# Router logits of a fused attention and mixture-of-experts kernel: from split weights on the full array to fp32 on four column tiles

## The chip, the cores and the metric

The kernel runs on one core of one Trainium2 chip. The metric is the device time of one execution in microseconds (us). Before the change it is 520.21 us, the median of three runs (519.32 to 525.32).

## The reference

An attention with pooled keys and values makes x, a two-level router picks one of 16 experts for each row of x, and that expert's two matrices are applied. Everything is fp32.

```python
k_p = k.reshape(B, H, Sp, 8, D).mean(axis=3)      # B=8, H=8, S=576, D=64, Sp=72
v_p = v.reshape(B, H, Sp, 8, D).mean(axis=3)
attn = softmax(q @ k_p.T / sqrt(D));  x = (attn @ v_p) as [B*S, 512]
g_logits = x @ w_group                            # 4 groups, argmax g, softmax weight g_w
e_logits = x @ w_expert[g]                        # 4 experts in the group, argmax e, weight e_w
out[row] = g_w * e_w * (relu(x @ w1[g, e]) @ w2[g, e])   # w1 512x1024, w2 1024x512
```

## The kernel before, in words

The work goes by batch (8 of 576 rows). For each batch, `Att` makes x transposed, in two halves of the rows (256 and 320 columns in batches 0 to 2, 288 and 288 later), and `Moe` runs one expert over the whole batch: the one that most rows chose, or for batches 0 and 1 a guess. Rows that chose another expert are placed by `Left` at the end, in blocks of 32; the first block is written out within the last batch, a loop at the end (L935) runs for the others, and the profiled execution takes no turn of it.

Every large matrix product is made in a one-pass fp32 form (fp32r) from a rounded high part and a low part that holds the rest: high by high, high by low, low by high. `cast` (L552, ScalarE) makes the high part of a weight chunk and `lo` (L557, GpSimd or VectorE) the low one. `av` (L383) makes x of a half in four PSUM banks, from which ScalarE writes the high part xt[:, 0] and `avd` (L401, VectorE) the low part xt[:, 1]. `up` (L567) is x by w1 with 12 matmuls a piece, ScalarE's relu and `upd` (L582, VectorE), which writes the low part of the hidden layer; `down` (L594) is the product by w2 in pieces of 8 matmuls of 512 columns. `up` and `down` share three PSUM buffers ("mm", pool ps_m).

The router: `rt` (L405) makes 20 logits from the weights wrs, which hold 20 high and 20 low columns, by eight fp32r matmuls a half that add up in PSUM; ScalarE copies 40 rows to lt; `route_g` (L432) transposes lt by five TensorE instructions, and two VectorE reductions add the two kinds of columns. `route_e` makes the choice oh, on GpSimd where its argument is "p", and `count` (L456) adds it up on TensorE.

What sets the order: each engine runs its instructions in the order of the plans START, FIRST, SECOND, STEADY and LAST (L36 to L77), lists of pieces. `m.` is the expert work of the batch, `n.` and `a.` the attention of the next and the first batch, `x.` the one after, `w.` the next expert's weights, `l.` the leftover rows; FIRST runs batch 0 with the attention of batch 1, SECOND batch 1, STEADY batches 2 to 6, LAST batch 7. All engines follow the plan (MANUAL, L78), but ScalarE's order in LAST is left to a scheduler. An instruction that waits holds all behind it on its engine. In FIRST GpSimd folds the values of batch 1 (`n.vr`, `n.vm`: lines 274 to 292), which `guess_x` (L480, TensorE) reads to guess batch 1's expert.

Of the kernel before, what the change touches and what calls it, by code (L numbers as in the profile page):

```python
# [69 lines left out]
m.load:2:3 m.lo:1:2:v l.step l.step m.load:2:2 m.up:0:0 p.tail m.up:0:1 m.upd:0:1 m.upd:0:0 l.step l.step l.step m.up:1:0 m.up:1:1 m.upd:1:0  # L70
l.step l.step l.step l.step l.xtiles m.upd:1:1 m.up:2:0 l.step l.step l.step l.step m.upd:2:0 l.step l.step m.up:2:1 m.upd:2:1 l.step
m.up:3:0 m.up:3:1 m.up:5:0 m.upd:3:0 l.step m.lo:1:3 m.upd:3:1 m.up:4:0 l.step l.which m.upd:4:0 m.split:2:2:v m.upd:5:0 m.split:2:1:v
m.up:6:0 m.upd:6:0 m.up:5:1 m.up:4:1 m.up:6:1 m.split:2:0 l.fetch_x l.tiles m.upd:5:1 m.upd:4:1 m.upd:6:1 l.slots m.down:0 m.down:1 l.fetch_a:1
# [891 lines left out]
```

## Time and profile before

| what | us |
|---|---|
| median of three runs | 520.21 |
| the profiled execution, its own time | 520.39 |
| its span, first to last instruction | 518.7 |
| TensorE matmul busy in the span | 502.9 (97%) |
| VectorE, ScalarE, GpSimd busy | 329.5, 206.3, 255.5 |
| granted TensorE clock, mean over the span | 0.996 |

PE is TensorE, DVE VectorE, ACT ScalarE, POOL GpSimd, SP the queue that issues most DMAs. A matmul's duration runs into the next one's, so a piece of PE work is measured here from its first start to the start of the next piece. An fp32 matmul that is not a transpose stands in the trace as two instructions.

### The profile page before, as it was taken

The numbers are of one execution on the slowest core, as the hardware profiler recorded it, in microseconds if no ns is written. First come the engines' busy times: TensorE is split into PE (matmuls) and PEld (weight loads), VectorE is DVE, ScalarE is ACT, GpSimd is POOL, SyncE is SP. The second block draws the span as 40 slices with busy tenths as digits, with TensorE's granted clock in tenths as the row PEclk, the third lists the DMA queues.
The fourth block names the chain that finished last, engine by engine and source line by source line (L and its number), as shares of the span: only waits on it lengthen the run. The fifth ranks groups of instructions, "written<-read, shape, count | busy, mean of one in ns | idle before, by whom it ended". The sixth has DMA issues, their size and how long they took to land.

```text
span 518.7 us, 14903 instructions
## 1 busy us (share of the span) xinstructions
PE 502.9 (97%) x6061; PEld 444.4 (86%) x6061; DVE 329.5 (64%) x928; ACT 206.3 (40%) x384; POOL 255.5 (49%) x235
## 2 busy tenths in 40 slices
PE   8799999999999999999999999999999999999995
PEld 7698877998789988898889988898889988889874
DVE  6887878798385765486664766385664763278602
ACT  2454342544226441545244542455334551344211
POOL 2394766565518632785049541685148760322400
PEclk9999999999999999999999999999999999999998
DMA  8699298585337942778164941997356101834741
GB/s 282 185 265 196 55 261 230 106 211 127 63 122 238 257 79 86 240 232 139 38 201 159 263 74 46 346 324 133 57 163 195 56 3 38 274 105 178 239 153 37
DMA packets 118126, 83.74 MB, mean 161 GB/s; under 512 B 71034, under 2 KB 93818, under 8 KB 117800
## 3 DMA queue, kind: packets, MB, share of 16 engines
q1 hardware_dynamic: 113424, 75.70, 54.3%
q10 hardware_dynamic: 4600, 7.02, 3.9%
q8 instruction: 49, 0.80, 0.7%
q14 instruction: 21, 0.17, 0.1%
q0 software_dynamic: 32, 0.04, 0.0%
HBM read 77.31 MB, written 28.53 MB: 204 GB/s over the span
## 4 chain that ended last, share of the span: by engine, by line
PE 81%; DVE 7%; DMA 4%; ACT 2%; POOL 2%; issue 1%; SPq 1%; DVEq 0%; ACTq 0%; POOLq 0%
PE mm L578 32%; PE mm L605 29%; PE mm L622 5%; PE sc L394 4%; PE sc L334 4%; PE tp L412 3%; DMA sw<-in_moe_w_dram 3%; DMA vv<-in_v_dram 1%; POOL w L561 1%; ACT w L555 1%; POOL p L373 1%; DVE pT L380 1%; DVE mx L346 1%; DVE p L355 1%; PE tp L436 1%
## 5 line engine op out<-in xcount | busy, mean ns | idle before, releaser
L605 PE MATMUL mm<-w,ht 128*128 128x512 f32 x768 | 177.4, 383 | 0.0
L561 POOL TENSOR_TENSOR w<-sw,w 128x1024 fp32r<-128x1024 f32 (+2 forms) x87 | 149.1, 1732 | 44.0 <-ACT w L555 39.7
L605 PEld LDWEIGHTS mm<-w,ht 128*128 128x128 f32 x768 | 141.4, 189 | 21.8 <-issue 1.6
L578 PE MATMUL mm<-xb,w 128*128 128x288 f32 (+1 forms) x768 | 109.5, 294 | 1.6 <-issue 0.8
L578 PEld LDWEIGHTS mm<-xb,w 128*128 128x128 f32 x768 | 100.6, 189 | 5.2 <-ACT w L555 2.2
L578 PE MATMUL mm<-xa,w 128*128 128x288 f32 (+1 forms) x768 | 100.8, 283 | 1.7 <-ACT xa L399 0.8
L578 PEld LDWEIGHTS mm<-xa,w 128*128 128x128 f32 x768 | 95.5, 190 | 4.8 <-issue 1.7
L580 ACT ACTIVATE ht<-mm 128x288 fp32r<-128x288 f32 (+2 forms) x128 | 51.8, 410 | 88.2 <-PE mm L578 86.7
L555 ACT CAST w<-sw 128x1024 fp32r<-128x1024 f32 x64 | 66.6, 1041 | 29.6 <-DMA sw<-in_moe_w_dram 27.3
L373 POOL TENSOR_TENSOR p<-p,su 128x864 f32<-128x864 f32 (+2 forms) x30 | 40.3, 1344 | 69.8 <-DVE su L368 54.0
L591 DVE SCALAR_TENSOR_TENSOR ht<-mm,ht 128x64 fp32r<-128x64 f32 (+4 forms) x192 | 37.9, 252 | 29.9 <-ACT ht L580 29.8
L616 ACT ACTIVATE y<-mm,gm 128x512 f32<-128x512 f32 x31 | 21.2, 685 | 70.8 <-PE mm L605 70.8
L513 POOL TENSOR_TENSOR mp<-oh,moh 128x80 f32<-128x80 f32 x8 | 2.8, 355 | 84.9 <-DVE moh L478 81.5
L360 ACT ACTIVATE p<-p 128x864 f32<-128x864 f32 (+2 forms) x30 | 23.4, 781 | 36.2 <-DVE p L355 31.0
L380 DVE STREAM_TRANSPOSE pT<-p 128x960 f32<-128x960 f32 (+2 forms) x30 | 29.2, 975 | 8.6 <-POOL p L373 7.9
L586 DVE SCALAR_TENSOR_TENSOR ht<-mm,ht 128x288 fp32r<-128x288 f32 (+1 forms) x64 | 27.0, 423 | 10.8 <-ACT ht L580 10.8
L366 DVE TENSOR_REDUCE s<-p 128x12 f32<-128x864 f32 (+2 forms) x30 | 25.8, 861 | 7.0 <-ACT p L360 7.0
L334 PEld LDWEIGHTS sc<-kT,qT 64*32 64x32 f32 x2176 | 23.6, 105 | 7.0 <-issue 4.0
L334 PE MATMUL sc<-kT,qT 64*32 64x72 f32 x2176 | 28.5, 229 | 1.1 <-DVE qT L320 1.1
L622 PE MATMUL mm<-w,ht 128*128 128x512 f32 x128 | 29.4, 381 | 0.0
L394 PE MATMUL sc<-pT,v 32*64 32x288 f32 (+2 forms) x384 | 26.9, 409 | 1.2 <-DVE pT L380 1.2
L346 DVE TENSOR_REDUCE mx<-sc 128x12 f32<-128x864 f32 (+2 forms) x28 | 24.3, 868 | 5.6 <-PE sc L334 5.6
(212 smaller groups left out, 523.0 us busy)
## 6 DMA issues: line engine op xcount, KB each, us to landing
sw<-in_moe_w_dram SPq DMA_DIRECT2D x72, 512.0 KB
vv<-in_v_dram SPq DMA_DIRECT2D x27, 320.0 KB
q<-in_q_dram SPq DMA_DIRECT2D x112, 72.0 KB
kv<-in_k_dram SPq DMA_DIRECT2D x14, 512.0 KB
out_dram<-y ACTq DMA_DIRECT2D x23, 256.0 KB
xscr<-xa SPq DMA_DIRECT2D x5, 1152.0 KB
xscr<-xb SPq DMA_DIRECT2D x5, 1152.0 KB
pT<-xscr SPq DMA_DIRECT2D x4, 1152.0 KB
```

What stands on the lines that cost most here:

```text
L334: nc.tensor.matmul(ps[x][32 * g:32 * g + 32, SP * t:SP * t + SP], lhsT=s.qT[c][64 * x:64 * x + 64, g, 32 * t:32 * t + 32], rhs=s.kT[64 * x ...
L346: red(out=m[:, x, 0:w], in_=ps[:, :, 0:SP * w].rearrange("p x (t s) -> p x t s", s=SP), axis=AX.X, op=ALU.max)
L373: (nc.vector if eng == "v" else nc.gpsimd).tensor_tensor(out=p, in0=p, in1=bc(s.su[c][:, 0:w], SP), op=ALU.mult)
L380: nc.vector.transpose(out=s.pT[:, :, o:o + n].rearrange("p j (t i) -> p t j i", i=32), in_=probs[:, z:z + n // 32].rearrange("p t (j i) -> ...
L394: nc.tensor.matmul(banks[a][64 * x:64 * x + 64, 0:n], lhsT=s.v6[32 * a:32 * a + 32, 5 if x and i == 0 else j, :], rhs=s.pT[32 * a:32 * a + ...
L555: nc.scalar.copy(out=s.w[m, j][0], in_=raw)
L561: (nc.vector if eng == "v" else nc.gpsimd).tensor_tensor(out=wl[:, i:i + n], in0=s.raw[m, j][:, i:i + n], in1=wh[:, i:i + n].bitcast(F32), ...
L578: nc.tensor.matmul(ps[:, 0:n], lhsT=l[:, kc, fs], rhs=apart(s.a.xt[hf][:, r, kc]), start=(kc == 0 and i == 0), stop=(kc == 3 and i == 2))
L580: nc.scalar.activation(out=halves(ht[:, sl]), in_=joined(ps[:, 0:n]), func=AF.Relu)
L591: stt(out=ht[:, at:at + hi - lo], in0=ps[:, a, lo:hi], scalar=0.0, in1=ht[:, t + lo:t + hi].bitcast(F32), op0=ALU.max, op1=ALU.subtract)
L605: nc.tensor.matmul(ps, lhsT=s.ht[f][:, 640 * l + o:640 * l + o + 128], rhs=apart(s.w[2, f // 2][r][:, f % 2, :]), start=(i == 0), stop=(i ...
L622: nc.tensor.matmul(ps, lhsT=s.ht[f][:, 512:640], rhs=apart(s.w[2, f // 2][r][:, f % 2, :]), start=(i == 0), stop=(i == 15))
```

## The change

The router's weights stay fp32 and padded to 32 columns a tile (wr, 128x4x32). `rt` makes, for each of the four 128-row chunks of x, one fp32 matmul on its own 32 columns of the array, without adding up: four matmuls a half in place of eight. They read xr, a new fp32 copy of x. `route_g` transposes lt as five full 128x128 blocks into two PSUM tiles and VectorE adds the four chunks.

In batches 1 to 7 `avd` writes x to xr straight from PSUM, and a new piece `xlo` on GpSimd makes the low part as xr minus the high part. In batch 0 `avd` makes the low part as before, and `xlo` on GpSimd makes xr as high plus low. The piece that split the router's weights goes, the pool of pT has one buffer instead of two, and two small memsets are new on GpSimd.

ScalarE's order in LAST is written out: each `split` becomes a `cast` and a `lo`. `p.tail`, the last rows of the batch before, comes after the first two pieces of `up`. The last chunk of the last batch (`ending`) is made as two halves of 256 columns, one after the other, each scaled by ScalarE and stored. The final loop stands in an If.

```diff
-t.warm:10 t.turn_wr a.kr:0 a.kr:1 t.split_wr a.kt ...
+t.warm:10 t.turn_wr a.kr:0 a.kr:1 a.kt ...
 ...
-m.up:5:0 a.pt:4 n.vr:0 m.upd:5:0 ... m.up:7:0 a.av:1 n.vr:1 n.vm a.rt:0 m.upd:7:0 a.avd:1 n.kr:0
-m.up:0:1:1 m.upd:0:1 n.kr:1 a.rt:1 n.guess_x ...
+m.up:5:0 a.pt:4 n.vr:0 a.xlo:0 m.upd:5:0 ... m.up:7:0 a.av:1 n.vr:1 n.vm a.rt:0 m.upd:7:0 a.avd:1 a.xlo:1 n.kr:0
+m.up:0:1:1 m.upd:0:1 n.kr:1 n.guess_x m.cast:2:0 m.up:1:1 a.rt:1 n.guess_e ...
 ...
-MANUAL = [{ET.PE, ET.SP, ET.DVE, ET.Activation, ET.Pool}, {ET.PE, ET.SP, ET.DVE, ET.Pool}]
+MANUAL = {ET.PE, ET.SP, ET.DVE, ET.Activation, ET.Pool}
 ...
-    wr = keep.tile([128, 4, 20], F32, name="wr")
-    wrs = keep.tile([128, 4, 40], F32R, name="wrs")
+    wr = keep.tile([128, 4, 32], F32, name="wr")
+    nc.gpsimd.memset(wr, 0.0)
+    lt = keep.tile([128, 640], F32, name="lt")
+    nc.gpsimd.memset(lt[:, S:640], 0.0)
 ...
-    pp = ctx.enter_context(tc.tile_pool(name="pp", bufs=2))
+    pp = ctx.enter_context(tc.tile_pool(name="pp", bufs=1))
 ...
         def avd(s, h):
+            o, n = s.half[h]
             for ps, g in s.ta[h]:
-                stt(out=s.xt[h][:, 1, g], in0=ps, scalar=0.125, in1=s.xt[h][:, 0, g].bitcast(F32), op0=ALU.mult, op1=ALU.subtract)
+                if s.b == 0:
+                    stt(out=s.xt[h][:, 1, g], in0=ps, scalar=0.125, in1=s.xt[h][:, 0, g].bitcast(F32), op0=ALU.mult, op1=ALU.subtract)
+                else:
+                    ts(out=s.rawt()[:, g, o:o + n], in0=ps, scalar1=0.125, scalar2=None, op0=ALU.mult)
+
+        def xlo(s, h, eng="p"):
+            o, n = s.half[h]
+            x, hi = s.xt[h], s.xt[h][:, 0].bitcast(F32)
+            e = nc.vector if eng == "v" else nc.gpsimd
+            if s.b == 0:
+                e.tensor_tensor(out=s.rawt()[:, :, o:o + n], in0=hi, in1=x[:, 1].bitcast(F32), op=ALU.add)
+            else:
+                e.tensor_tensor(out=x[:, 1], in0=s.rawt()[:, :, o:o + n], in1=hi, op=ALU.subtract)
 
         def rt(s, h):
 ...
-            for i in range(8):
-                nc.tensor.matmul(ps[0:40, 0:n], lhsT=wrs[:, i // 2, :], rhs=apart(s.xt[h][:, i % 2, i // 2]), start=(i == 0), stop=(i == 7))
-            nc.scalar.copy(out=halves(s.lt[0:40, sl]), in_=joined(ps[0:40, 0:n]))
+            for a in range(4):
+                nc.tensor.matmul(ps[32 * a:32 * a + 32, 0:n], lhsT=wr[:, a, :], rhs=s.xr[:, a, o:o + n], start=True, stop=True)
+            nc.scalar.copy(out=lt[:, o:o + n], in_=ps[:, 0:n])
 ...
-            for c, (o, n) in enumerate(CH):
-                nc.tensor.transpose(out=lp[0:n, 40 * c:40 * c + 40], in_=s.lt[0:40, o:o + n], identity=ident[0:40, 0:40])
+            lp = [ps_t.tile([128, 512], F32, name="tp") for i in range(2)]
+            for c in range(NC):
+                nc.tensor.transpose(out=lp[c // 4][:, 128 * (c % 4):128 * (c % 4) + 128], in_=lt[:, 128 * c:128 * c + 128], identity=ident)
 ...
+            if s.b == B - 1 and c == 3:
+                return s.ending(o, t)
 ...
-                if s.b == B - 1 and c == 3:
-                    ts(out=y[:, 256:512], in0=joined(ps)[:, 1], scalar1=s.a.gm[:, c:c + 1], scalar2=None, op0=ALU.mult)
-                    nc.scalar.activation(out=y[:, 0:256], in_=joined(ps)[:, 0], func=AF.Copy, scale=s.a.gm[:, c:c + 1])
 ...
+            for i in range(16 * t, 16 * t + 16):
+                a, (f, l, r) = i // 24, ops[i % 24]
+                nc.tensor.matmul(s.pe[a][:, 0:256], lhsT=s.ht[f][:, 640 * l + o:640 * l + o + 128], rhs=apart(s.w[2, f // 2][r][:, f % 2, 256 * a:256 * a + 256]),
+                                 start=(i % 24 == 0), stop=(i % 24 == 23))
+                if i % 24 == 23:
+                    part = s.ye[:, 256 * a:256 * a + 256]
+                    nc.scalar.activation(out=halves(part), in_=joined(s.pe[a][:, 0:256]), func=AF.Copy, scale=s.a.gm[:, 3:4])
+                    (nc.sync if a else nc.scalar).dma_start(out=out[S * s.b + o:S * s.b + o + 128, 256 * a:256 * a + 256], in_=part)
 ...
-    with tc.For_i(0, nit, 1):
-        left.block()
+    with tc.If(nit > 0):
+        with tc.For_i(0, nit, 1):
+            left.block()
```

On TensorE in FIRST, from the second `av` of batch 0 (L394, L395 in the new file) to the transposes of its logits; L412 is `rt` before and L428 after, L484 and L499 `guess_x`. Before:

```order
L394 MATMUL tp<-pT,v_341 64x320 x4
L412 MATMUL tp<-xa,wrs 40x256 x8
L578 MATMUL mm<-xb,w 128x320 x12
L412 MATMUL tp<-xb,wrs 40x320 x8
L484 MATMUL tp<-heads,v_741 64x4 x10
L578 MATMUL mm<-xb,w 128x320 x12
L492 MATMUL tp<-wr,gx 128x20 x4
```

and with the change:

```order
L395 MATMUL tp<-pT,v_341 64x320 x4
L428 MATMUL tp<-xr,wr 32x256 x4
L593 MATMUL mm<-xb,w 128x320 x12
L499 MATMUL tp<-heads,v_741 64x4 x10
L593 MATMUL mm<-xb,w 128x320 x12
L428 MATMUL tp<-xr,wr 32x320 x4
L507 MATMUL tp<-wr,gx 128x20 x4
```

The second `rt` moved behind the guess and one piece of `up`; the first one stayed, and now reads xr.

On GpSimd at the same place (L275 to L293 in the new file are the folds of batch 1's values, L420 is `xlo` of batch 0), with the change:

```order
L275 TENSOR_TENSOR vv<-vv 128x2x256
L276 TENSOR_TENSOR vv<-vv 128x2x128
L288 TENSOR_TENSOR v_741<-vv 128x128
L420 TENSOR_TENSOR xr<-xa 128x4x256
L275 TENSOR_TENSOR vv<-vv 128x3x256
L276 TENSOR_TENSOR vv<-vv 128x3x128
L288 TENSOR_TENSOR v_741<-vv 128x192
L293 TENSOR_TENSOR v_741<-v_741,share 128x64 x2
L420 TENSOR_TENSOR xr<-xb 128x4x320
L469 TENSOR_TENSOR oh<-o_930,o_964 128x80
```

Without the two rows of L420 the row order is that of before: the first stands ahead of the second fold, the second behind it.

On VectorE at the start of LAST (L640 and L666 are the tail's addition, the next four lines `upd` of the first two pieces). Before:

```order
L698 COPY kv<-tp 128x320 x2
L640 TENSOR_TENSOR y<-mm,y 64x512
L591 SCALAR_TENSOR_TENSOR ht<-mm,ht 128x144
L591 SCALAR_TENSOR_TENSOR ht<-mm,ht 128x80
L591 SCALAR_TENSOR_TENSOR ht<-mm,ht 128x64
L586 SCALAR_TENSOR_TENSOR ht<-mm,ht 128x288
```

and with the change:

```order
L724 COPY kv<-tp 128x320 x2
L606 SCALAR_TENSOR_TENSOR ht<-mm,ht 128x144
L606 SCALAR_TENSOR_TENSOR ht<-mm,ht 128x80
L606 SCALAR_TENSOR_TENSOR ht<-mm,ht 128x64
L601 SCALAR_TENSOR_TENSOR ht<-mm,ht 128x288
L666 TENSOR_TENSOR y<-mm,y 64x512
```

The tail's addition, which empties a PSUM buffer, went behind the three and one instructions that empty the two of `up`.

## Rows read from the trace of the kernel before

**Rows 1.** The page: busy time of each engine, share of the span, instructions.
```profile
PE 502.9 (97%) x6061; PEld 444.4 (86%) x6061; DVE 329.5 (64%) x928; ACT 206.3 (40%) x384; POOL 255.5 (49%) x235
```
**Rows 2.** Windows over one steady batch: busy by engine, clock, DMA share, GB/s.
```profile
243.90:277.60 33.70, 33.70 (x310) 28.94 (x311) 18.64 (x56) 11.69 (x22) 12.45 (x10) 1.00 0.45 127
277.60:302.50 24.90, 24.90 (x410) 23.56 (x408) 17.96 (x41) 13.32 (x23) 18.12 (x13) 1.00 0.80 202
```
**Rows 3.** Timeline of PE, the router's matmuls in a steady batch: start, duration, instruction.
```profile
248.58 1.17 PE L412 MATMUL tp<-xa,wrs 128*40 128x288 f32 x8
249.59 1.89 PE L605 MATMUL mm<-w,ht 128*128 128x512 f32 x8
251.32 1.14 PE L412 MATMUL tp<-xb,wrs 128*40 128x288 f32 x8
252.30 3.62 PE L605 MATMUL mm<-w,ht 128*128 128x512 f32 x16
```
**Rows 4.** Timeline of PE in LAST: fp32 matmuls on four column tiles.
```profile
497.53 1.93 PE L844 MATMUL tp<-sw,q 128*32 128x256 f32 x32
499.40 0.92 PE L605 MATMUL mm<-w,ht 128*128 128x512 f32 x3
```
**Rows 5.** Timeline of PE: the logits' transposes, and five full ones of the keys.
```profile
255.85 0.47 PE L436 MATMUL tp<-ident,lt 40*128 40x40 f32 x5
256.25 0.48 PE L605 MATMUL mm<-w,ht 128*128 128x512 f32 x1
...
263.49 0.60 PE L297 MATMUL tp<-ident,kb 128*128 128x128 f32 x4
...
263.95 0.46 PE L605 MATMUL mm<-w,ht 128*128 128x512 f32 x1
```
**Rows 6.** Timeline of POOL in FIRST.
```profile
40.68 1.82 POOL L274 TENSOR_TENSOR vv<-vv 128x768 f32<-128x768 f32 x1
...
44.77 0.81 POOL L292 TENSOR_TENSOR v<-v,share 128x64 f32<-128x64 f32 x2
54.45 0.33 POOL L454 TENSOR_TENSOR oh<-o,o 128x80 f32<-128x80 f32 x1 [8.87 <-DVE o L425]
```
**Rows 7.** Groups of POOL's instructions over the span: shape, count, busy us, mean ns.
```profile
L561 POOL TENSOR_TENSOR w<-sw,w 128x1024 fp32r<-128x1024 f32 x43 | 102.8, 2397 | 34.9 <-ACT w L555 34.9
```
**Rows 8.** Timeline of PE in FIRST, the same stretch.
```profile
41.18 1.07 PE L412 MATMUL tp<-xa,wrs 128*40 128x256 f32 x8
...
44.03 1.25 PE L412 MATMUL tp<-xb,wrs 128*40 128x320 f32 x8
45.21 0.95 PE L484 MATMUL tp<-heads,v 128*64 128x4 f32 x20
```
**Rows 9.** Timeline of PE: the second `av` of batch 1 and the wait before it.
```profile
86.19 0.50 PE L394 MATMUL sc<-pT,v 32*64 32x320 f32 x4 [1.15 <-DVE pT L380]
```
**Rows 10.** Timeline of POOL, the end of FIRST.
```profile
90.49 1.68 POOL L275 TENSOR_TENSOR vv<-vv 128x384 f32<-128x384 f32 x1
...
96.81 0.33 POOL L454 TENSOR_TENSOR oh<-o,o 128x80 f32<-128x80 f32 x1 [2.84 <-DVE o L425]
```
**Rows 11.** Timeline of PE at the start of SECOND.
```profile
96.69 2.84 PE L578 MATMUL mm<-xa,w 128*128 128x256 f32 x24
99.37 0.35 PE L459 MATMUL tp<-oh,ones 128*128 128x80 f32 x2
```
**Rows 12.** Timeline of PE, ACT and DVE at the start of LAST.
```profile
456.42 1.71 PE L578 MATMUL mm<-xa,w 128*128 128x288 f32 x12
456.53 0.41 ACT L580 ACTIVATE ht<-mm 128x288 fp32r<-128x288 f32 x1
...
456.97 0.59 DVE L591 SCALAR_TENSOR_TENSOR ht<-mm,ht 128x144 fp32r<-128x144 f32 x3 [0.70 <-ACT ht L580]
```
**Rows 13.** Timeline of all engines, the end.
```profile
512.37 0.48 DVE L611 TENSOR_SCALAR y<-mm,gm 128x256 f32<-128x256 f32 x1 [1.26 <-PE mm L605]
...
512.88 0.47 ACT L612 ACTIVATE y<-mm,gm 128x256 f32<-128x256 f32 x1 [3.65 <-DVE y L611]
```

More of the change, by code (lines that the diff above doesn't have):

```diff
@@ L62 @@
 m.up:4:0 m.upd:4:0 n.ex:2 m.up:4:1 m.upd:4:1 n.su_:2 n.nm:2:p x.load_qb:0 x.load_qb:1 m.up:5:0 m.upd:5:0 m.cast:2:2 m.lo:2:2 m.up:5:1 m.upd:5:1 n.pt:2
-x.load_qb:2 x.load_qb:3 m.up:6:0 m.upd:6:0 m.up:7:0 m.cast:2:3 m.lo:2:3 m.upd:7:0 n.av:0 n.avd:0 m.up:6:1 m.upd:6:1
-m.up:7:1 m.upd:7:1 n.av:1 n.rt:0 n.avd:1
+x.load_qb:2 x.load_qb:3 m.up:6:0 m.upd:6:0 m.up:7:0 m.cast:2:3 m.lo:2:3 m.upd:7:0 n.av:0 n.avd:0 n.xlo:0 m.up:6:1 m.upd:6:1
+m.up:7:1 m.upd:7:1 n.av:1 n.rt:0 n.avd:1 n.xlo:1
 m.down:0 n.rt:1 x.kr:0 m.down:1 x.kr:1 m.down:2 n.route m.down:3 m.down:4 m.down:5 n.main_expert w.load:1:0 w.load:1:1 w.load:1:2 w.load:1:3
@@ L69 @@
 LAST = """
[L70 to L73, printed above, removed]
+m.load:2:3 m.lo:1:2:v l.step l.step m.load:2:2 m.up:0:0 m.up:0:1 m.upd:0:1 m.upd:0:0 p.tail l.step l.step l.step m.up:1:0 m.up:1:1 m.upd:1:0
+l.step l.step l.step l.step l.xtiles m.upd:1:1 m.up:2:0 m.cast:2:1 l.step l.step l.step l.step m.upd:2:0 l.step l.step m.up:2:1 m.upd:2:1 l.step
+m.up:3:0 m.up:3:1 m.up:5:0 m.upd:3:0 l.step m.lo:1:3 m.cast:2:2 m.upd:3:1 m.up:4:0 l.step l.which m.upd:4:0 m.lo:2:2:v m.upd:5:0 m.lo:2:1:v
+m.up:6:0 m.cast:2:0 m.upd:6:0 m.up:5:1 m.up:4:1 m.up:6:1 m.lo:2:0 m.cast:2:3 l.fetch_x l.tiles m.upd:5:1 m.upd:4:1 m.upd:6:1 l.slots m.down:0 m.down:1 l.fetch_a:1
 m.up:7:0 l.fetch_b:1 m.upd:7:0 l.whole:4 l.whole:0 m.up:7:1 l.rows l.next_ l.whole:3 m.upd:7:1 l.turn:3 l.turn:4 m.down:12
-l.whole:1 l.turn:1 l.turn:0 l.whole:2 m.split:2:3:p m.down:2 m.down:3 l.turn:2 m.down:4 l.gather m.down:5 l.back m.down:6 l.up m.down:7 l.hback
+l.whole:1 l.turn:1 l.turn:0 l.whole:2 m.lo:2:3:p m.down:2 m.down:3 l.turn:2 m.down:4 l.gather m.down:5 l.back m.down:6 l.up m.down:7 l.hback
 m.down:8 l.down l.fetch_x l.fetch_a l.fetch_b m.down:13 m.down:9 m.down:10 l.slots m.down:11
 """
-MANUAL = [{ET.PE, ET.SP, ET.DVE, ET.Activation, ET.Pool}, {ET.PE, ET.SP, ET.DVE, ET.Pool}]
+MANUAL = {ET.PE, ET.SP, ET.DVE, ET.Activation, ET.Pool}
 @with_exitstack
@@ L633, in down, with ending @@
                 s.store(c, "a")
+        def ending(s, o, t):
+            ops = [(f, l, r) for f in range(8) for l, r in ((0, 0), (0, 1), (1, 0))]
+            if t == 0:
+                s.pe = [ps_m.tile([128, 512], F32, name="mm") for i in range(2)]
+                s.ye = sm.tile([128, DM], F32, name="y")
+            for i in range(16 * t, 16 * t + 16):
[6 more added lines that the diff above has]
+                    (nc.sync if a else nc.scalar).dma_start(out=out[S * s.b + o:S * s.b + o + 128, 256 * a:256 * a + 256], in_=part)
         def tail(s):
@@ L784, in xtiles @@
         def xtiles(s):
-            s.xh = [pp.tile([128, 5, S], F32, name="pT")[:, 0:NG] for i in range(2)]
+            s.xh = [pp.tile([128, 5, S], F32, name="pT")[:, 0:NG], xp.tile([128, NG, S], F32, name="xr")]
             for t in s.xh:
@@ L924, in run @@
                 getattr(who[who_], fn)(*[int(z) if z.isdigit() else z for z in args])
-    with tc.manual_schedule(engines=MANUAL[0]):
+    with tc.manual_schedule(engines=MANUAL):
         run(START, 0)
```

40 lines of the change are left out of this document (16 added, 24 removed).

## The prediction

> **What bounds the kernel now.** First the page's busy shares: TensorE is busy 502.9 of 518.7 us, no other engine over 64% [rows 1]. Busy matmul time alone proves little, so the second view is the windows over one steady batch: in both stretches TensorE is busy for the whole window at full granted clock, while VectorE has 36.6 of 58.6 us and GpSimd 30.6 [rows 2]. Third, the timeline of starts: eight `down` matmuls take 1.73 us from first start to the next piece, 0.216 each, and pieces follow without a gap [rows 3]. So TensorE's own work sets the time, and a change counts by what it takes off TensorE and by the waits it puts in front of TensorE. For the waits I read GpSimd's timeline in FIRST, where it is the engine that others wait for.
>
> The profiled execution took 520.39 us and the median is 520.21, so the two may be used alike; the sum is made from 520.39.
>
> **Part 1, the logits' matmuls.** A half's eight matmuls take 1.01 us (248.58 to 249.59) and 0.98 us (251.32 to 252.30), 0.1225 each [rows 3]. The trace has the new form elsewhere: 128x32 fp32 matmuls with 256 columns in the leftover block, 16 of them (32 records) in 1.87 us from first start to the next piece [rows 4], so four, one per column tile, take 0.47 us, and at 288 columns 0.53. That they run side by side is in that number: one fp32 matmul of 256 columns alone cannot be 0.117 us if a one-pass one of 288 takes 0.1225. The lower bound is four of the old matmuls, 0.49 us. The upper bound takes the price of a change of tile shape on top: 16 `down` matmuls ahead of the 40-row transposes take 3.55 us (252.30 to 255.85), where 16 at 0.216 are 3.46 [rows 3, 5], so 0.09 more, 0.62 us a half. But the eight `down` ahead of the old logits, whose tile is narrow too, paid nothing (1.73 us for eight, 249.59 to 251.32) [rows 3]. I take 0.55. Saved: 0.995 less 0.55, times 16 halves, **7.1 us** (bounds 6.0 and 8.1). All of it is on the path, since TensorE has no gaps there.
>
> On this the Trainium skill, "TensorEngine Tiling (Array Packing)", Key Properties, says that a change of the tiling mode, not only of the tile, drains the engine. By that rule every half would pay, 0.62 us, and the saving would be 6.0 us. The trace agrees for one of the two narrow shapes and disagrees for the other.
>
> **Part 2, the transposes.** Five of 40 rows take 0.40 us and pay the 0.09 of their shape; five full ones take 0.46 us (263.49 to 263.95) [rows 5]. Per batch 0.03 less, 0.2 us in all. VectorE's two reductions read twice the elements, some tenths of a us a batch, with 22 us idle in a steady batch [rows 2]; counted at nothing. `avd` loses its wait for ScalarE; its durations stay about the same; nothing.
>
> **Part 3, `xlo` on GpSimd.** 1024 elements a partition take 2.40 us there, 2.34 ns each [rows 7]. A pair is 2.7 us twice in the steady batches, 5.4 on 30.6 us in 58.6 [rows 2]: hidden, as the next batch's `up` reads the low part a whole `down` later. If that cover went, it would show as `up` waiting for GpSimd.
>
> In FIRST it isn't hidden. GpSimd is on a row without idle until 44.77 + 0.81 = 45.58 us and only then idle for 8.87 us [rows 6].
> - The first `rt` stands at 41.18 us [rows 8] and reads xr, which `xlo` starts at 40.7, behind the first fold [rows 6], and ends at 43.1: TensorE waits 1.9 us, and all of `up` behind it.
> - The rest of the folds ends 2.4 us later, at 48.0. `guess_x` stood at 45.21 [rows 8], behind an `rt` of 1.18 us that is now behind it. TensorE would come to it at 45.21 + 1.9 - 1.2 - 0.4 = 45.5 and stick in its middle until 48.0: 2.1 us.
> - The second `rt` waits for the `xlo` of 1280 elements, 3.0 us from 48.0, so until 51.0. TensorE is there after the end of the guess (0.6) and one piece of `up` (1.75), at 50.4: 0.6 us.
>
> Together **+4.6 us**. These waits are new, on the path, and a good half of the saving. They are least if GpSimd is faster next to an idle VectorE, and bounds are half of that and one and a half times, 2.3 and 6.9.
>
> At the end of FIRST both `xlo` of batch 1, 5.4 us, stand ahead of the last fold and of oh, which `count` waits for. GpSimd idled 2.84 us before oh at 96.81 [rows 10], and `count` at 99.37 came 2.2 us after oh was done [rows 10, 11]. 5.4 - 2.84 - 2.2: **+0.4 us** (0 to 2.5).
>
> The second `av` of batch 1 waited 1.15 us for its probabilities [rows 9]. It now comes one `down` piece and more later, 1.73 us [rows 3], so this wait goes: **-1.2 us** (0 to -1.2).
>
> **Part 4, LAST.** The first two pieces of `up` and the tail hold the three PSUM buffers. Before, the tail's addition freed one and the third piece began at 456.42 [rows 12]. Now the buffer freed first is that of the second piece, and its relu stands on ScalarE behind a weight cast, at 456.53; VectorE then needs until 456.97 + 0.59 = 457.56 [rows 12]. **+1.2 us** for TensorE (0 if ScalarE comes to it earlier).
>
> **Part 5, the end.** 48 matmuls of 256 columns in place of 24 of 512: 24 of 256 columns took 2.68 us (96.69 to 99.37) [rows 11], so 5.36 against 24 x 0.216 = 5.19: +0.2. Behind the last matmul VectorE's half ran first and ScalarE's after it, 0.48 and 0.47 us [rows 13]; now one eviction of that size is left, -0.5. The store is as long as it was. The branch around the loop takes the place of the loop's own test; nothing. The early split of the weights, two small instructions beside DMA waits, and the two memsets: nothing. One pT buffer: its next writer comes after the last reader in every plan; nothing.
>
> **Sum:** 520.4 - 7.1 - 0.2 + 4.6 + 0.4 - 1.2 + 1.2 + 0.2 - 0.5 = **517.8 us**.
>
> **Rivals.**
> *The new waits don't bind.* If xr of batch 0 is ready in time, or TensorE's later pieces make up for it, parts 3 and 4 lose 4.6 + 0.4 + 1.2: 511.6 us. For it: VectorE's and ScalarE's waits in FIRST give back some of any delay. Against: GpSimd's rows leave no hole before 45.58 us [rows 6].
>
> *GpSimd slows down beside VectorE.* 384 elements took 1.68 us while VectorE folded keys, 4.4 ns each, almost twice the usual [rows 10, 7]. If every `xlo` in FIRST ran so, they would last 4.5 and 5.6 us: the guess 2.1 us later, the second `rt` another 2.6, `count` up to 2.5: 517.8 + 7.2 = 525.0 us. For it: this row, at the very place. Against: it is the slowest of its kind, and the folds in FIRST's middle ran at 2.4 ns (1.82 us for 768) [rows 6]. The Trainium skill, "GPSIMD Engine Reference", Specifications, says that GpSimd shares its SBUF interfaces with VectorE and contends with VectorE instructions that have two SBUF inputs; the slow row, beside the fold of two SBUF inputs, agrees.
>
> *The four column tiles run one after the other.* Slower: each matmul of a half would take the 0.53 us of the group, 2.1 us a half, 1.1 more than now, and the sum 517.8 + 16 x (2.1 - 0.55) = 542.6 us. It decides from 0.995 us a half on. Against: rows 4 are this very form, with the tiles in the same rotation. For it only that here each tile has one matmul, not four in succession, in a group.
>
> **How the numbers follow.** Forecast 0.64, no new waits 0.16, slow GpSimd 0.16, tiles in series 0.04. The forecast's own bounds: best 517.8 - 1.0 - 2.3 - 0.4 - 1.2 = 512.9; worst 517.8 + 1.1 + 2.3 + 2.1 + 1.2 = 524.5; not all ends at once, so some 514 to 522. To leave out no more than 2 in 10 the range is 513.0 to 522.5, which takes in the near part of both middle rivals. Two per cent is about what a measurement of this kernel can tell from no change: below 509.8 faster, 0.05 (the first rival with the best price of part 1); above 530.6 slower, 0.05; within, 0.90.
>
> **What would show it.** In the new profile: L428 pieces of about 0.55 us from start to the next piece, 0.5 us off each of two a batch, and a steady batch (58.6 us before) at 57.7; waits of TensorE's L428 and L499 for POOL L420 and L293 in FIRST, near 2 us each; no wait of the second L395 of batch 1; a wait for VectorE at the third piece of `up` in LAST; one ScalarE eviction after the last matmul. Wrong would be the forecast if L428 takes over 0.7 us, if steady batches wait for L422, or if FIRST ends as early as before.

## The result, and the profile after

The changed kernel takes **526.73 us** (median of 5 runs, 525.91 to 530.25) against 520.01 for the kernel before in the same session (5 runs): the ratio is 1.0134, 95% interval 1.0104 to 1.0165. That is slower by more than the uncertainty, though inside 2%. The prediction was 517.8 us, 513.0 to 522.5: the wrong sign, outside the range. The profiled execution is the median one, 526.73 us with a span of 525.0.

The page of the changed kernel, busy time by engine, against [rows 1]:

```profile
PE 504.8 (96%) x6085; PEld 440.3 (84%) x6085; DVE 348.5 (66%) x926; ACT 207.1 (39%) x384; POOL 300.6 (57%) x253
```

GpSimd has 45 us more, which is `xlo`. VectorE has 19 us more, though the change gave it hardly more work: the logits' reductions take 1.7 us more, and `avd` as long as before. What grew is the folds of the keys: the same instructions take 19.6 us longer. That is the first thing to ask about. Where the time went is read from the first `up` matmul of each batch, from the timelines of both kernels:

| starts, us | before | after | later by |
|---|---|---|---|
| batch 0 | 25.98 | 27.34 | 1.4 |
| batch 1 | 96.69 | 101.20 | 4.5 |
| batch 2 | 158.61 | 168.69 | 10.1 |
| batch 3 | 218.07 | 227.45 | 9.4 |
| batch 7 (LAST) | 452.87 | 460.87 | 8.0 |
| end of span | 518.7 | 525.0 | 6.2 (518.71, 524.95) |

So START to SECOND lose 10 us, and everything from batch 2 on gains: 0.42 a batch on average over batches 2 to 6 (0.34 over 3 to 6), 1.8 in LAST.

TensorE's waits over the span (us in total, times, longest):

```profile
PE tp L474 <- POOL oh L469: 3.1, 1, 3.1
PE mm L335 <- ACT qT L316: 2.2, 1, 2.2
PE tp L298 <- DVE kb L271: 2.0, 2, 1.1
PE mm L593 <- issue: 1.9, 2, 1.0
PE tp L428 <- POOL xr L420: 1.9, 1, 1.9
PE mm L593 <- DVE ht L606: 1.4, 1, 1.4
...
PE tp L499 <- POOL v L293: 0.9, 1, 0.9
```

The waits of L428, L499 and L606 were forecast, at 1.9, 2.1 and 1.2. The 3.1 of `count` (L474) was forecast at 0.4, and L298's wait for VectorE's `kb` not at all. VectorE and GpSimd at the end of FIRST, which answer to [rows 10]:

```profile
96.30 1.15 DVE L275 TENSOR_TENSOR kv<-kv 128x768 f32<-128x768 f32 x1
97.48 3.16 DVE L276 TENSOR_TENSOR kv<-kv 128x384 f32<-128x384 f32 x1
100.67 2.06 DVE L271 TENSOR_TENSOR kb<-kv 128x384 f32<-128x384 f32 x1
102.66 0.48 DVE L454 TENSOR_REDUCE lg<-tp 128x80 f32<-128x320 f32 x1
```

```profile
96.60 3.63 POOL L422 TENSOR_TENSOR xb<-xr,xb 128x1280 fp32r<-128x1280 f32 x1
100.18 2.14 POOL L275 TENSOR_TENSOR vv<-vv 128x768 f32<-128x768 f32 x1
...
106.78 0.33 POOL L469 TENSOR_TENSOR oh<-o,o 128x80 f32<-128x80 f32 x1 [1.77 <-DVE o L441]
```

The fold of 384 elements takes 0.56 us on VectorE where GpSimd is quiet. Here it takes 3.16 and ends 0.4 us after GpSimd's `xlo` ends (100.23). The next one takes 2.06 and ends 0.4 us after GpSimd's own fold (102.32). So **a VectorE fold stands still beside the GpSimd instruction that is running**, 4.1 us in two folds; the routing behind them starts at 102.66 though its transposes were done at 99.4. GpSimd itself is idle for 1.77 us ahead of `oh`: it waits for VectorE, not the other way round. What TensorE sees:

```profile
99.39 1.97 PE L633 MATMUL mm<-w,ht 128*128 128x512 f32 x8
101.20 2.84 PE L593 MATMUL mm<-xa,w 128*128 128x256 f32 x24
107.16 0.71 PE L474 MATMUL tp<-oh,ones 128*128 128x80 f32 x2 [3.12 <-POOL oh L469]
```

The same in SECOND, where the fold of 256 elements, 0.42 us otherwise, takes 3.02 beside `xlo`, and TensorE's transposes of the keys are later by 1.1 us (timelines of VectorE, GpSimd and TensorE):

```profile
148.99 3.02 DVE L276 TENSOR_TENSOR kv<-kv 128x256 f32<-128x256 f32 x1
```

```profile
148.44 3.29 POOL L422 TENSOR_TENSOR xb<-xr,xb 128x1280 fp32r<-128x1280 f32 x1 [0.77 <-DVE xr L413]
```

```profile
158.11 0.44 PE L298 MATMUL tp<-ident,kb 128*128 128x128 f32 x2 [1.10 <-DVE kb L271]
```

In the steady batches it happens too (2.75 us in each, 0.42 where GpSimd is quiet) and TensorE has no wait that follows from it. The second surprise is the granted clock. In three stretches it is at 1.2 GHz, half, behind idle time of TensorE (2.2 us at 20.50, 1.9 at 44.12, 3.1 at 107.16); before, it fell only at the end. Windows of the changed kernel (length, busy by engine, clock, DMA share, GB/s):

```profile
21.70:25.20 3.50, 3.50 (x10) 2.50 (x8) 2.52 (x6) 2.40 (x3) 2.69 (x5) 0.51 1.08 358
45.60:52.50 6.90, 5.98 (x39) 5.54 (x38) 6.80 (x8) 1.54 (x3) 6.50 (x6) 0.51 1.07 183
107.00:110.50 3.50, 3.34 (x14) 3.34 (x15) 2.39 (x9) 3.06 (x7) 1.62 (x5) 0.51 0.16 37
```

In the steady batches the logits answer to [rows 3]:

```profile
258.41 0.69 PE L428 MATMUL tp<-xr,wr 128*32 128x288 f32 x8
259.03 1.99 PE L622 MATMUL mm<-w,ht 128*128 128x512 f32 x8
260.95 0.69 PE L428 MATMUL tp<-xr,wr 128*32 128x288 f32 x8
261.58 3.72 PE L622 MATMUL mm<-w,ht 128*128 128x512 f32 x16
265.13 0.71 PE L452 MATMUL tp<-ident,lt 128*128 128x128 f32 x5
```

A half takes 0.62 us from first start to the next piece, and the eight `down` between the two take 1.92, where [rows 3] have 1.73. From the first logits to the transposes it is 6.72 us, 7.27 before: 0.55 a batch gained, not 0.89. Of these, 0.12 a batch go again in the middle of `up`, in waits that the profile puts down to issue (0.92 and 0.96 us in batches 3 and 5, 0.58 and 0.82 before), and 0.07 in the transposes, from their first start to the next piece 0.47 us, 0.40 before.

### The profile page after: what moved, and what is told of

The parts are those of the page before. It is cut to its first block, busy times and chain, and to the rows that moved or that the text cites. A ratio compares the mean times of both kernels' runs of the same rounds, so it can differ in the third digit from the quotient of the medians.

```text
span 525.0 us, 14915 instructions
## 1 busy us (share of the span) xinstructions
PE 504.8 (96%) x6085; PEld 440.3 (84%) x6085; DVE 348.5 (66%) x926; ACT 207.1 (39%) x384; POOL 300.6 (57%) x253
## 4 chain that ended last, share of the span: by engine, by line
PE 80%; DVE 9%; POOL 4%; ACT 2%; issue 2%; DMA 2%; SPq 0%; ACTq 0%; DVEq 0%; POOLq 0%
PE mm L593 32%; PE mm L622 27%; PE sc L335 5%; PE mm L633 4%; PE sc L395 4%; PE tp L428 1%; DVE kv L276 1%; PE mm L654 1%; DMA pT<-in_k_dram 1%; PE mm L933 1%; POOL p L374 1%; POOL w L576 1%; DVE xr L413 1%; DMA sw<-in_moe_w_dram 1%; PE tp L298 1%
## 5 line engine op out<-in xcount | busy, mean ns | idle before, releaser
L622 PE MATMUL mm<-w,ht 128*128 128x512 f32 x744 | 172.8, 385 | 0.0
L622 PEld LDWEIGHTS mm<-w,ht 128*128 128x128 f32 x744 | 136.8, 189 | 26.0 <-issue 7.6
L593 PE MATMUL mm<-xb,w 128*128 128x288 f32 (+1 forms) x768 | 112.5, 300 | 1.0 <-issue 1.0
L593 PEld LDWEIGHTS mm<-xb,w 128*128 128x128 f32 x768 | 103.6, 193 | 5.8 <-ACT w L570 2.2
L606 DVE SCALAR_TENSOR_TENSOR ht<-mm,ht 128x64 fp32r<-128x64 f32 (+4 forms) x192 | 37.7, 251 | 33.4 <-ACT ht L595 33.4
L633 PE MATMUL mm<-w,ht 128*128 128x512 f32 x128 | 29.6, 382 | 0.0
L633 PEld LDWEIGHTS mm<-w,ht 128*128 128x128 f32 x128 | 23.9, 189 | 3.9 <-issue 0.7
```

Of the source, the lines that this page charges most:

```text
L593: nc.tensor.matmul(ps[:, 0:n], lhsT=l[:, kc, fs], rhs=apart(s.a.xt[hf][:, r, kc]), start=(kc == 0 and i == 0), stop=(kc == 3 and i == 2))
L606: stt(out=ht[:, at:at + hi - lo], in0=ps[:, a, lo:hi], scalar=0.0, in1=ht[:, t + lo:t + hi].bitcast(F32), op0=ALU.max, op1=ALU.subtract)
L622: nc.tensor.matmul(ps, lhsT=s.ht[f][:, 640 * l + o:640 * l + o + 128], rhs=apart(s.w[2, f // 2][r][:, f % 2, :]), start=(i == 0), stop=(i ...
L633: nc.tensor.matmul(ps, lhsT=s.ht[f][:, 512:640], rhs=apart(s.w[2, f // 2][r][:, f % 2, :]), start=(i == 0), stop=(i == 15))
```

## The experiments

Theory A came out of these rows: GpSimd's `xlo` costs FIRST and SECOND, in its own queue and by holding VectorE. The rivals were the clock, the routing moved one piece later, and the later batches. Medians of 6 to 12 runs are given, and the ratio to runs of the kernel before in the same session, with its 95% interval. Each expectation letters its own theories. The edits are given in short, with what is left out marked by dots or told in words. Where two runs of different sessions are compared, the difference of the medians stands first; the ratios take out what differs between sessions.

**xlo_vector.** `a.xlo:0` to `a.xlo:0:v`, and so for all six in FIRST and SECOND: VectorE makes them.

> The changed kernel with all six xlo of START, FIRST and SECOND (batches 0 to 2) issued on VectorE instead of GpSimd; the steady batches keep GpSimd. Theory A (GpSimd's xlo are what FIRST and SECOND lose: TensorE waits for them in GpSimd's queue, and VectorE's folds stand still while one runs): the wait of L428 for GpSimd (1.9 us at 44.12), the VectorE folds of 3.0 to 3.2 us, the wait of count (3.1 us) and that of L298 in SECOND (1.1 us) go or shrink to under 1 us, and with them two of the three stretches at half clock (6.8 and 3.4 us, 5 us lost); VectorE has six pieces of 1.1 to 1.4 us more. Time 517 to 521 us, against 526.7. Rival B (the low part costs the same wherever it is made, because VectorE's own queue is then late): within 1.5 us of 526.7, with the waits now for VectorE. Rival C (the loss is in START, LAST and the steady batches): FIRST gets shorter by its waits of some 5 us alone, with clocks as they were, 522 us or more.

523.96 us, 1.0063 (1.0035 to 1.0092): 2.8 us less (3.7 by the ratios), short of theory A's 517 to 521. The wait for xr is gone, and others took its place:

```profile
PE tp L499 <- POOL v L293: 3.0, 1, 3.0
PE tp L474 <- POOL oh L469: 2.1, 1, 2.1
```

TensorE now meets `guess_x` (L499) earlier, and GpSimd's folds that it needs end only 0.4 us earlier, since the hold works the other way as well. Beside VectorE's `xlo` a fold on GpSimd that takes 0.65 us in the changed kernel takes 1.72, and ends 0.45 us after the `xlo`:

```profile
44.65 2.16 DVE L420 TENSOR_TENSOR xr<-xb 128x1280 f32<-128x1280 f32 x1
```

```profile
45.54 1.72 POOL L288 TENSOR_TENSOR v<-vv 128x192 f32<-128x192 f32 x1
```

`count` still waits, for the routing on a VectorE that has the six pieces as well. Theory A and rival B are each half right here. The time lies in rival C's interval, and the three stretches at half clock are still there, so this run alone does not rule C out; late_only does.

**fill_waits.** Unused matmuls in the waits:

```
+ def fill(ps, z): z fp32 matmuls, 256 columns, into the waiting piece's own PSUM tile
- a.sc:2:m  a.rt:0  n.guess_x  a.count (batch 1)
+ a.sc:2:m:3  a.rt:0:4  n.guess_x:2  a.count:6
```

> The changed kernel with unused matmuls of the warm-up kind (128x128, 256 columns, fp32, 0.5 us each) put in front of the waiting matmuls, into the same PSUM tile that these write afterwards: 3 ahead of the scores in START's gap at 20.50, 4 ahead of the first rt, 2 ahead of guess_x of batch 1, 6 ahead of batch 1's count. The waits stay as long as they were, TensorE only works through them. Theory A (the granted clock fell to 1.2 GHz because TensorE stood idle there, and some 6 us of the loss is the clock behind the waits, not the waits): full clock in all three stretches (21.7, 45.6 and 107.1 us), 519.5 to 522 us. Rival B (the waits themselves are the whole loss): no faster than 526, and up to 1 us slower where the matmuls run past the end of a wait. Rival C (the clock falls there for something other than the idle time): the stretches at 1.2 GHz stay, 526 to 528.

525.35 us, 1.0089 (1.0056 to 1.0121). The clock is full in all three stretches (its mean over the span is 0.993 to 1.0 in the 8 runs, 0.986 to 0.990 in the changed kernel's 5), so idle time did bring it down; but only 1.4 us came back (2.3 by the ratios, whose intervals overlap) where theory A said 5 to 7. The second `rt` shows why:

```profile
52.54 0.75 PE L435 MATMUL tp<-xr,wr 128*32 128x320 f32 x8 [1.28 <-POOL xr L426]
```

At full clock TensorE is early and waits for xr, whose `xlo` ends at 52.5 (48.82 + 3.67) whatever the clock. In FIRST, GpSimd sets the time and the slow clock was hidden behind it: batch 0's `up` starts 1.3 us earlier than in the changed kernel, batch 1's only 0.3. My theory of the clock fell.

**no_branch.**

```
-     with tc.If(nit > 0):
-         with tc.For_i(0, nit, 1):
+     with tc.For_i(0, nit, 1):
```

> The changed kernel without the branch around the leftover loop (the loop's own test alone, as before). Theory A (what the end gained beyond the 0.5 us of one eviction is the loop's bookkeeping that the branch skips: from the last store's issue to the end 5.3 us before, 3.7 now): 1.2 to 1.8 us slower, 528.2. Rival (the last store is faster because it is on the other queue): within 0.3 us of the changed kernel.

527.40 us, 1.0138 (1.0094 to 1.0182): by the timed runs not told apart from the changed kernel. In the trace the stretch from the last store's issue to the end is 5.76 us (521.44 to 527.2), 3.67 with the branch (521.28 to 524.95), 5.3 before (513.39 to 518.7). The one trace agrees with theory A; the times fit neither theory's interval and don't settle it.

**rt_adjacent** and **rt_twice** ask what the logits cost.

```
- n.av:1 n.rt:0 n.avd:1 n.xlo:1 m.down:0 n.rt:1 x.kr:0 m.down:1 x.kr:1
+ n.av:1 n.avd:1 n.xlo:1 m.down:0 x.kr:0 m.down:1 n.rt:0 n.rt:1 x.kr:1
```

> The changed kernel with both rt of a steady batch side by side, behind the second down piece, in place of one ahead of the first down piece and one behind it. Theory A (entering and leaving the four column tiles costs TensorE 0.1 us each way: eight down matmuls between the two rt take 1.92 us where eight take 1.73): 0.2 us less a batch, 1 to 1.4 us in six, 525.5. Rival B (the price lies in the four matmuls themselves, 0.62 us a half): no difference beyond 0.3 us. Rival C (the routing starts later and something waits for it): slower by 0.5 us or more.

526.67 us, 1.0109 (1.0062 to 1.0155): no difference that the runs resolve. In the trace both halves together take 1.11 us:

```profile
263.94 1.18 PE L428 MATMUL tp<-xr,wr 128*32 128x288 f32 x16
265.05 1.99 PE L622 MATMUL mm<-w,ht 128*128 128x512 f32 x8
```

```
-            for a in range(4):
+            for a in list(range(4)) * (2 if s.b > 2 else 1):
```

> The changed kernel with the four logits' matmuls of a half issued twice, from batch 3 on; only the duration of L428 is of interest. A half took 0.62 us from its first start to the next piece, where 0.55 was forecast. Theory A (the unit is 0.47 x 288/256 = 0.53 us and 0.1 us is the price of entering the tiles): twice gives 1.15 us. Rival B (0.62 is what four such matmuls take): 1.24 us. Rival C (the second four overlap the first, being on the same tiles with weights loaded ahead): under 1.05 us.

In a single run (531.2 us), one half twice takes 1.11 us as well.

```profile
259.96 1.18 PE L428 MATMUL tp<-xr,wr 128*32 128x288 f32 x16
261.07 1.99 PE L622 MATMUL mm<-w,ht 128*128 128x512 f32 x8
```

Four more matmuls cost 0.49 us, so 0.13 of the 0.62 is paid once at entry, whether the second four are the same half or the other; and the eight `down` between two halves take 0.2 more than eight alone. The bare price is 0.49, the forecast's lower bound; with the entry it is 0.62, its upper one.

**late_only** puts START and FIRST of before back, with the old logits for batches 0 and 1; the rest is as changed.

```
- START, FIRST of the changed kernel       + START, FIRST of before, split_wr, wrs
- if s.b == 0: stt(...)      (avd)         + if s.b < 2: stt(...)
+ rt, route_g: if s.b < 2, the code of before
```

> START and FIRST of the kernel before, word for word, with the old logits (eight one-pass matmuls on 40 rows, no xlo) for batches 0 and 1; everything else as in the changed kernel: the new logits, the moved pieces and GpSimd's xlo from batch 2 on, LAST, the split last chunk, the branch. Theory A (what the change loses, it loses in FIRST and around its end, where steps were moved and GpSimd's and VectorE's work lies on the path; from batch 2 on it gains 0.3 to 0.55 us a batch, and 2 us at the end): batch 1's up starts where it did before (96.7 us), no stretch at half clock, one wait of 1.1 us in SECOND left; faster than before by 2 to 4 us, 516 to 518 us. Rival B (the new logits lose in the steady batches too, and FIRST only shows it first): no faster than before, 520 or more. Rival C (START's and FIRST's order was not the cause, the clock was): half clock returns somewhere and the time is 523 or more.

**517.16 us**, 0.9910 (0.9880 to 0.9941): faster than before by 0.9%, and 9.6 us less than the changed kernel (11.6 by the ratios). So the steady batches, LAST and the end gain, and the loss is all in front of them. Theory A.

**xlo_pieces.**

```
-                e.tensor_tensor(out=x[:, 1], in0=s.rawt()[:, :, o:o + n], in1=hi, op=ALU.subtract)
+            for g in range(NG): e.tensor_tensor(out=x[:, 1, g], in0=s.rawt()[:, g, o:o + n], in1=hi[:, g], ...)
```

> The changed kernel with each xlo issued as four GpSimd instructions, one per column group, in place of one (256 to 320 elements a partition each, 0.65 to 0.8 us). Theory A (a VectorE fold whose operands both lie in SBUF stands still until the GpSimd instruction that is running ends; it takes 2.75 to 3.1 us instead of 0.42 beside one xlo): no fold of 256 elements over 1.4 us, count's wait of 3.1 us at the end of FIRST down to 1.5 or less, L298's wait in SECOND under 0.5; and rt's first matmul waits for a quarter only. 522 to 525 us. Rival B (GpSimd's and VectorE's rates go down in proportion while both run): folds and waits as long as before, 526 to 527 us. Rival C (four instructions cost GpSimd more than one): its queue gets later, 527.5 or more.

524.34 us, 1.0067 (1.0042 to 1.0091), in theory A's interval. The two folds of 384 elements beside `xlo` at the end of FIRST take 0.97 and 1.11 us, L298's wait in SECOND is down to 0.24; but `count` still waited 2.6 us, against theory A's 1.5. The hold moved behind: VectorE's timeline, and GpSimd's,

```profile
102.22 1.54 DVE L442 TENSOR_TENSOR o<-r,m 128x20 f32<-128x20 f32 x1
```

```profile
101.90 1.82 POOL L275 TENSOR_TENSOR vv<-vv 128x768 f32<-128x768 f32 x1
...
106.41 0.33 POOL L470 TENSOR_TENSOR oh<-o,o 128x80 f32<-128x80 f32 x1 [0.16 <-DVE o L442]
```

Twenty elements, 0.18 us, held for the rest of a GpSimd fold. The length of the GpSimd instruction is what counts, not how much VectorE has to do. The hold is not all of this wait: GpSimd idles only 0.16 us ahead of `oh`, because its four pieces take 3.77 and 3.97 us where one instruction took 2.55 and 3.63. Its own queue has become nearly as late as VectorE.

**late_fix** moves batch 2's second `xlo` in SECOND behind `gates`.

```
- n.avd:1 n.xlo:1 m.down:4 ... n.gates n.gm_
+ n.avd:1 m.down:4 ... n.gates n.xlo:1 n.gm_
```

> late_only with one step moved in SECOND: the second xlo of batch 2 goes from behind avd to behind gates, past the fold of batch 3's keys on VectorE. Theory A (that fold stands still for 2.6 us beside xlo, and TensorE's transposes of the keys wait 1.1 us for it): the wait is gone, 0.8 to 1.2 us less than late_only, 515 to 517. Rival (the fold is late for another reason): no difference beyond 0.3 us. Rival (xlo is now late for batch 2's up): slower than late_only.

517.20 us, 0.9929 (0.9895 to 0.9963): nothing gained. The wait at L300 (L298 in the changed kernel) went from 1.07 us to 0.23, as theory A had it, and 24 us later TensorE waits for VectorE's transpose of q instead (0.17 in late_only):

```profile
172.58 1.21 PE L337 MATMUL sc<-kT,qT 64*32 64x72 f32 x96 [0.93 <-DVE qT L323]
```

The wait was real and not the last one on the path.

**old_batch0** and **old_batch1b** split the 9.6 us: late_only with one of the two batches in the changed form, its lines of FIRST with it.

```
- if s.b < 2 (rt, route_g, avd)     + old_batch0: b == 0;  old_batch1b: rt, route_g for b == 1
  FIRST: old_batch0 lines 1-5 of before, then changed; old_batch1b the reverse
```

> late_only with batch 1 in the changed kernel's form again: old logits and FIRST's first five lines of before for batch 0 alone; batch 1 has the new logits, its xlo on GpSimd at the end of FIRST, and its second av, its rt and its routing one down piece later, as in the changed kernel. With the next kernel this splits the 9.5 us between late_only (517.2) and the changed kernel (526.7). Theory A (both places lose: about 4 us in batch 0's part by the ledger of up starts, 4 to 5 us around batch 1's count): 521 to 522.5 us, with count waiting 2 to 3 us for oh and the fold of 384 elements at 3 us, and half clock behind it. Rival B (batch 0's part is the whole loss, and the end of FIRST was only late because of it): 517 to 518. Rival C (the end of FIRST is the whole loss): 525 or more.

> late_only with batch 0 in the changed kernel's form: new logits for batch 0, GpSimd's xlo ahead of rt and between the folds, the first five lines of FIRST as in the changed kernel; batch 1 with the old logits and the end of FIRST as before. Theory A (batch 0's part is what is left of the 9.5 us once batch 1's 4.1 are taken off): L428's wait of 1.9 us for xr, guess_x's for GpSimd, batch 1's up 3.5 to 5 us later than in late_only, 521 to 522.5 us. Rival B (the rest of FIRST absorbs most of it): under 519.

A first form of the second, old_batch1, has no time: its `avd` of batch 1 was the old one and that of batch 0 the new one, so nothing made the low part that batch 0's `xlo` reads.

521.30 us, 1.0016 (0.9991 to 1.0040), and 522.25 us, 1.0032 (1.0008 to 1.0056). Batch 1's part costs 4.1 us, batch 0's 5.1; 9.2 of 9.6 (by the ratios 5.5 and 6.3, of 11.6). Neither absorbs the other. In old_batch0 `count` waits 3.0 us and the two folds take 3.15 and 2.07 as above; in old_batch1b L435 waits 1.9 for xr and L514 1.9 for GpSimd's folds.

**folds_behind** and **folds_in_pieces** leave the routing where the change put it and take the holds away in two steps.

```
- n.xlo:0 n.xlo:1 x.kr:1 x.vr:1 x.vm x.load_qb:1 ... n.gates n.gm_:p m.store:4     (from old_batch0)
+ n.xlo:0 n.xlo:1 x.kr:1 x.load_qb:1 ... n.gates n.gm_:p x.vr:1 x.vm m.store:4
  folds_in_pieces: and xlo in four, as in xlo_pieces
```

> old_batch0 with one step moved: GpSimd's second fold of batch 2's v (x.vr:1, x.vm, 4.7 us) from ahead of batch 1's oh to behind it. The routing stays one down piece later than before. Theory A (VectorE stands still beside whatever GpSimd instruction is running: its fold of 384 elements was held until 96.3 by xlo, the next until 98.4 by GpSimd's own fold, and the routing began 3.2 us after its transposes): the second hold goes, the first stays; count waits 1 to 1.8 us instead of 3.0; 519.5 to 520.5 us. Rival B (the routing that was moved one piece later is the cause): the wait stays at 2.5 or more, 521. Rival C (GpSimd's queue ahead of oh is the cause): the wait goes altogether.

> folds_behind with each xlo issued as four GpSimd instructions. Theory A: no VectorE fold over 1.4 us at the end of FIRST, count waits at most 0.3 us though the routing stays where the change put it, no stretch at half clock behind it, L298's wait in SECOND gone: 517 to 518.5 us, as late_only, which has batch 1's old logits. Rival B (the later routing): count still waits 2 us or more, 520 or more.

519.88 us, 0.9995 (0.9970 to 1.0019), and 517.78 us, 0.9949 (0.9926 to 0.9973). VectorE in the first, then in the second:

```profile
92.81 3.16 DVE L277 TENSOR_TENSOR kv<-kv 128x384 f32<-128x384 f32 x1
96.01 0.56 DVE L272 TENSOR_TENSOR kb<-kv 128x384 f32<-128x384 f32 x1
96.49 0.48 DVE L468 TENSOR_REDUCE lg<-tp 128x80 f32<-128x320 f32 x1
```

```profile
92.64 1.11 DVE L277 TENSOR_TENSOR kv<-kv 128x384 f32<-128x384 f32 x1
93.79 1.10 DVE L272 TENSOR_TENSOR kb<-kv 128x384 f32<-128x384 f32 x1
94.81 0.48 DVE L469 TENSOR_REDUCE lg<-tp 128x80 f32<-128x320 f32 x1
```

One hold less, then none of length. `count` waits 3.0, 1.0, 0.6 us in the three kernels, and batch 1's new logits then cost 0.6 us over late_only instead of 4.1 (by the ratios 2.0 instead of 5.5). The gain over both steps is clear of the intervals, that of the first step alone is not, and the second step takes L299's wait in SECOND too (1.07 to 0.23 us). The routing stayed one `down` piece later throughout, so that was not the main cause; what is left may be its share. In old_batch0 GpSimd idled 1.78 us ahead of `oh`, waiting for VectorE, so there its own queue was not the cause; but the first step also empties that queue, and without it the pieces would have made it late, as in xlo_pieces.

**late_tail**, **combined** and **best_of_all** add up what helped.

```
- m.load:2:2 m.up:0:0 m.up:0:1 m.upd:0:1 m.upd:0:0 p.tail     (LAST)
+ p.tail m.load:2:2 m.up:0:0 m.up:0:1 m.upd:0:1 m.upd:0:0
  combined: late_only, this, xlo_pieces, rt_adjacent;  best_of_all: folds_in_pieces, this, rt_adjacent
```

> late_only with one step moved in LAST: the tail of the batch ahead goes from behind the first two upd to the head of LAST, so that VectorE's addition frees its PSUM buffer ahead of everything. Theory A (the third up piece waits 1.4 us for the second piece's upd because the tail holds the third buffer): that wait goes, 0.5 us stays as a wait two pieces later (0.7 of it was given back in LAST before): 0.5 to 1.4 us less than late_only, 516.2. Rival (the third piece is not on the path, later waits take the time back): within 0.3 us of late_only.

> late_only with LAST's tail first, xlo in four instructions, and the two rt of a steady batch side by side: the version that the runs so far point to. Theory A (each gives what it gave by the trace: 0.5 to 1.2, up to 1, 0.13 a batch): 514.5 to 516 us. Rival (what is left hides behind the loads and VectorE): 516.5 to 517.5, as late_only.

> folds_in_pieces with LAST's tail first and the two rt of a steady batch side by side, as in combined. Theory A (batch 1's new logits and what was freed are worth 0.3 to 1 us over combined's 514.6): 513.5 to 515 us. Rival (SECOND takes it back, as it did with late_fix): 514.5 to 515.5.

515.65 us, 0.9903 (0.9868 to 0.9938); **514.60 us**, 0.9898 (0.9851 to 0.9945); 514.83 us, 0.9890 (0.9864 to 0.9916). With the tail first, LAST's third `up` piece no longer waits 1.4 us for `ht`. All three beat both kernels. By the ratios they can't be told apart from each other, nor from late_only (0.9910): their medians are 1.5 to 2.6 us lower than its, but whether the tail or the other edits add anything is inside the uncertainty.

## Why the prediction was wrong, by its own steps

**The step that failed is part 3's end of FIRST**, "5.4 - 2.84 - 2.2: +0.4", with the -1.2 for `av`. The +0.4 counted GpSimd's queue alone, and the -1.2 took it that nothing behind `av` would be late. `oh` was late because VectorE was, held by `xlo` and by GpSimd's fold: 4.1 us measured for the whole of batch 1's part (old_batch0; 5.5 by the ratios), where +0.4, -1.2 and its two halves of logits (-0.9) made -1.7. The row that showed it lay in front of me. [rows 10] have a GpSimd fold of 1.68 us, and I read it as GpSimd slowed by VectorE, the rival with 0.16; the VectorE fold beside it took 1.24 us in place of 0.56, and that half of the pair I did not look up. From the timeline of VectorE before:

```profile
91.34 1.24 DVE L275 TENSOR_TENSOR kv<-kv 128x384 f32<-128x384 f32 x1
```

I also had the wrong page with it: the Trainium skill's "GPSIMD Engine Reference", Specifications, says only that the two contend. The Trainium skill's "SBUF — State Buffer", SBUF: two separate sides, says that of a VectorE instruction with two SBUF inputs and a GpSimd instruction that reads SBUF, whichever starts first holds the shared ports for its whole instruction while the other is blocked. By that rule the forecast would have had two folds held here. folds_behind (the second fold 2.07 us to 0.56) and folds_in_pieces (the first 3.16 to 1.11) agree with it, and xlo_vector in the other direction (GpSimd's fold 0.65 us to 1.72).

That rival's sum, 525.0, came near the measured time by luck. It had every `xlo` in FIRST at 4.5 and 5.6 us; they took 2.35, 3.67, 2.55 and 3.63.

*Part 3, batch 0.* Its mechanism was right: L428 waited 1.89 us for xr (1.9 forecast) and `guess_x` for the folds (2.1 forecast; 1.9 in old_batch1b, 0.9 in the changed kernel, whose TensorE was late at half clock). Its size: 5.1 us net of two halves of logits (6.3 by the ratios), where 4.6 - 0.9 = 3.7 was forecast. The second `rt` came at 52.8 instead of 51: this part of FIRST ran 1.0 us later because of START, and the second `xlo` took 3.67 us and not 3.0.

*Part 1.* Mis-sized: 0.62 us a half, and 0.2 a batch on the `down` between. I chose 0.55 between bounds of 0.49 and 0.62. 0.55 a batch measured against 0.89, 2.7 us over eight, before the 0.12 a batch that the waits in `up` take. The Trainium skill's "TensorEngine Tiling (Array Packing)", Key Properties, has a change of tiling mode drain the engine; by that rule I had 0.62 and a saving of 6.0. The traces (0.13 at entry, 0.2 on the `down` between) agree with it, and my row against it, the old 40-row logits that paid nothing, was of another shape.

*Not forecast at all.* SECOND's 1.1 us for `kb`, the same hold. START's 1.4: the clock was at half from 21.7 on. late_fix, which has START of before, fell to half at 17.6, old_batch0 and combined, with it too, near 22, and late_only with the same START did not, so this belongs to the execution as much as to the change. The end: from the start of the `down` before the last chunk (505.15 and 513.39) to the end of the span 2.0 us less, against -0.3 forecast (the eviction and the narrower matmuls). By no_branch's trace this is the loop's bookkeeping, which the branch skips and part 5 put at "nothing"; its times don't settle it.

*Right.* LAST's wait was 1.44 us (1.2 forecast), of which 0.7 was given back a few pieces later, where TensorE had waited 0.7 us before (the piece at 464.80). The transposes cost 0.46 us. The second `av` of batch 1 waits no more, but the time was lost again behind it.

By the forecast's own list of what would prove it wrong, none of its three signs came: the unnamed one did.

## What to carry to other kernels

Before giving an engine hidden work, look up in the trace what its neighbours' instructions take beside it: here a filler instruction of 3 us on GpSimd was a stop of up to 2.6 us for a VectorE instruction with both operands in SBUF, and it cost nothing in the steady loop and all of it where VectorE was on the path. Cut such fillers short where their engine has time for it (four pieces took longer than one here), and place them past the chain that decides. Recover a clock or a wait only after asking what is late next: fill_waits and late_fix each took away a real loss, and the next wait took most of it back.

## What the runs showed of the hardware

- A VectorE instruction with two operands in SBUF does not get on while a GpSimd tensor_tensor runs: 0.42 to 0.56 us became 2.75 to 3.16, and 0.18 became 1.54. With GpSimd's work in quarters the folds of 384 took 0.97 to 1.11. VectorE's reads of PSUM at such times kept their 0.5 to 0.9 us.
- GpSimd is held as well: 1280 elements took 2.94 us beside no fold (151.78 in late_fix), and 3.67 and 3.63 where a VectorE fold had started just ahead (48.72 for 0.94 us, `xlo` at 48.74; 96.30 for 1.15 us, `xlo` at 96.60).
- Four fp32 matmuls on four column tiles: 0.49 us at 288 columns, 0.13 more at entry.
- After 1.9 to 3.1 us of idle TensorE the granted clock was at 1.2 GHz for 3.4 or 6.8 us; with matmuls in the same gaps it stayed at 2.4. The length of the gap alone doesn't tell: at the same place in START a gap of 1.85 us left the clock full (before), one of 1.76 did not (combined).
